# Loading q and k by pairs of tiles, eight tokens of a head to a partition, in a local-attention and maxout-FFN kernel

## The chip, the cores and the metric

The kernel runs on one core of one Trainium2 chip. The metric is the device time of one execution in microseconds. Engine names are those of the profile: PE (TensorE matmul), PEld (its weight loads), DVE (VectorE), ACT (ScalarE), POOL (GpSimd), SP (SyncE, which issues almost all DMA transfers).

## The reference

Inputs are q, k and v with 4 batches, 8 heads, 768 tokens and head size 64, and four FFN weights. Everything is fp32 at the borders.

```python
def _attn_ref(q, k, v, n_global, n_local):          # n_global = 8, n_local = 96
    scores = scale * np.matmul(q, k.transpose(0, 1, 3, 2))
    rel = pos[:, None] - pos[None, :]
    is_global = pos[None, :] < n_global
    is_local = (rel >= 0) & (rel < n_local)
    keep = is_global | is_local
    dist = np.where(is_global & ~is_local, n_local, np.abs(rel))
    slopes = 2.0 ** (-8.0 * (np.arange(H) + 1) / H)
    scores = scores - slopes[:, None, None] * dist
    scores = np.where(keep, scores, -1e9)
    a = softmax(scores)                             # written out in the original
    return np.matmul(a, v)

x = attn_out.transpose(0, 2, 1, 3).reshape(B * S, H * D)       # 3072 x 512
h = np.maximum(np.maximum(x @ w1, x @ w2), x @ w3)             # 3072 x 768
out = h @ w_out                                                # 3072 x 512
```

## The kernel before

**Tiles.** The 4 x 768 tokens are 24 tiles of 128 tokens, numbered 0 to 23, six to a batch. Because a query looks at its own and the 95 tokens before it, and at 8 global tokens, a tile's attention needs k and v of its own tile, of the tile before, and the batch's first 8 tokens. The FFN works on chunks of 4, 2, 2, 4, 4, 4, 4 tiles.

**Units and their order.** The program is a list of units, written out by hand in the string `SCHEDULE`. Each unit issues the instructions of one small step. Every engine, and the DMA queue of SP, executes its own instructions strictly in the order of this list, so a unit that waits holds back all that comes after it on the same engine. The letters that matter here (n is a number of a load group, s a part of it, T a tile, g a half of the heads, c a chunk, f a block of 128 FFN columns; the last number mostly chooses the engine for a copy: 0 ACT, 1 DVE, 2 POOL):

- `l n.s` (`load_part`): loads one part of q or k of a group of tiles in the first half of the kernel; the first two parts are loaded ahead of the list. `c n.s.how` (`cast_part`): casts it to bf16. `x n.s.how` (`u_x`): eight 128x128 PE transposes into PSUM and the copy to `qkT`, which holds q and k with the head dimension on partitions. On copies, 0 is ACT and 1 DVE with PSUM pool psT, 2 and 3 the same engines with pool psH, and 4 splits between both.
- `L T`, `C T.0.how`, `X T.how`: the same for one tile in the second half, with 256-byte rows; X with 4 is a DMA transpose. For C, 3 splits the cast between DVE and POOL.
- `v T` and `C T.1.how`: load and cast v. `G` and `V` put the 8 global tokens in place.
- `S T.g.how` (`u_S`): scores of four heads into PSUM and the exponential on ACT into `P`; with how = 1 the bias is added by PE matmuls, otherwise `M T.g` multiplies `P` by a mask on DVE. `B` and `K` make the bias and mask tables at the start.
- `A T.how` (`u_A`): probabilities times v on PE, then reciprocal and product on DVE into `xb`. `T T.how` (`u_XT`): transpose to `xT`, by PE or (4) by DMA.
- `w`, `W`, `o`, `Q`: load and cast the FFN weights. `F c.f.j` (`u_F1`): one FFN product of a chunk (four matmuls), read by ACT for j = 0 and by a maximum on DVE for j = 1 and 2. `O c.tt.how` (`u_F2`): output of one tile, six matmuls, copy and store. `E`: the last chunk's outputs. `D`: matmuls on zeros.

**Load groups.** Tiles 0 to 11 come in groups given by `GROUPS = [[0, 2], [2, 2], [4, 2], [6, 4], [10, 2]]` (first tile, number of tiles). Each part is 512 KB in one transfer; a partition takes 2 (or 4) neighbouring tokens of each of 8 (or 4) heads, so that a row in memory is 512 bytes (or 1 KB). The pool `raw` that receives q and k has 5 buffers.

**Heads.** Neighbouring heads 2j and 2j+1 share one 128-partition column block j of `qkT`, one in each half of the partitions.

**PSUM.** Pools are psS (score and output tiles, tags sp0 and sp1), psH (3 buffers for FFN products) and psT (1 buffer).

Of the kernel before, what the change touches and what calls it, by code (L numbers as in the profile page):

```python
# [25 lines left out]
    K6 K5 D1.2 D4.8 B2.1 B4.1 B7.1 B5.1 l1.0 l1.1 K4 B6.1 v0 B1.0 B3.1 c0.0.1 K1 K3 x0.0.2 K7 B0.1  # L26
    c0.1.1 x0.1.4 G0.2 c1.0.1 c1.1.1 K0 S0.0.1 S1.1.1 M1.1 S1.0.0 G1.2 x1.0.3 S0.1.1 x1.1.0 K2 M0.0
    C0.1.1 M0.1 A0.1 v1 C1.1.2 S2.0.0 M1.0 S2.1.0 G2.1 T0.1 M2.0 S3.0.0 S3.1.1 M3.1 v2 l2.0 c2.0.1
    M2.1 M3.0 C2.1.2 v3 A1.0 x2.0.2 V1.2 G3.2 A2.1 C3.1.2 T1.0 V2.2 l2.1 c2.1.1 A3.0 V3.0 w0.0 T2.0
    w0.1 x2.1.4 T3.1 W0.0.0 S4.0.0 W0.1.1 S4.1.0 w0.2 D3.1 F0.0.0 G4.1 M4.1 M4.0 F0.1.0 F0.1.1  # L30
    W0.2.0 F0.0.1 S5.1.0 w1.0 W1.0.0 W2.0.1 S5.0.0 F0.1.2 v4 C4.1.1 F0.0.2 M5.1 F0.4.0 w1.1 A4.1
    V4.1 W1.1.1 W2.1.1 w1.2 v5 F0.3.0 M5.0 F0.5.0 F0.2.0 F0.2.1 T4.1 F0.3.1 F0.4.1 W1.2.0 F0.2.2
    C5.1.2 A5.1 W2.2.0 F0.3.2 l3.0 F0.5.1 c3.0.0 T5.1 l3.2 c3.2.0 F0.5.2 x3.2.2 l3.1 c3.1.1 x3.0.1
    F1.4.0 F1.1.0 F1.0.0 l3.3 c3.3.0 o0 Q0.0 x3.1.3 F0.4.2 F1.0.1 x3.3.0 F1.2.0 G6.0 F1.2.1 F1.1.1
    l4.1 o1 S6.0.0 S6.1.0 v6 C6.1.2 Q1.1 F1.0.2 F1.5.0 F1.5.1 S7.0.0 S7.1.0 G7.1 F1.4.1 F1.5.2
    c4.1.1 F1.3.0 o2 Q2.0 F1.4.2 M7.1 v7 S8.0.0 M6.1 l4.0 c4.0.0 L12 L14 C7.1.2 v9 v8 L13 M7.0
    S8.1.0 F1.1.2 v11 O0.3.1 v13 v10 M6.0 A7.0 G8.2 F1.3.1 C12.0.0 O0.0.0 v12 x4.1.2 T7.1 A6.0
    O0.1.1 S9.1.0 S9.0.0 V7.1 M8.0 T6.0 x4.0.3 F1.2.2 M8.1 O0.2.1 M9.0 M9.1 C8.1.0 F2.5.0 F2.0.0
    G9.2 S10.0.0 S10.1.0 G10.2 F1.3.2 C9.1.2 F2.0.1 F2.0.2 A8.0 X12.0 F2.2.0 C13.0.3 V8.2 A9.1 X13.4
    T8.4 T9.4 F2.4.0 F2.5.1 C14.0.1 X14.4 v15 F2.4.1 S11.0.0 S11.1.0 O1.1.0 M11.0 M10.1 M10.0 F2.2.1  # L40
    S12.0.0 S12.1.0 F2.2.2 M11.1 F2.5.2 V9.2 C10.1.2 A10.0 V10.1 C11.1.2 L15 O1.0.0 F2.1.0 F2.4.2
    C13.1.2 A11.0 T10.0 F2.1.1 F2.3.0 S13.1.0 G12.0 S13.0.0 L18 T11.1 M12.1 F2.3.1 F2.3.2 M12.0
    G13.2 C15.1.2 L16 v14 C14.1.2 F3.5.0 F3.4.0 F3.4.1 F2.1.2 C12.1.0 M13.1 S14.0.0 M14.0 C15.0.0
    X15.4 S14.1.0 F3.5.1 M13.0 F3.1.0 A12.0 M14.1 F3.4.2 F3.2.0 F3.0.0 A13.0 V13.0 F3.1.1 C16.0.0
    G14.0 F3.2.1 F3.2.2 L19 F3.3.0 C18.0.0 X16.0 L17 F3.1.2 S15.1.0 S15.0.0 C19.0.1 T12.4 G15.0
    F3.3.1 F3.0.1 F3.0.2 X18.4 T13.4 C17.0.0 A14.1 F3.3.2 V14.1 F3.5.2 M15.0 X19.4 S16.0.0 L20 T14.4
    S16.1.0 M16.1 v18 C18.1.2 v17 v16 O2.0.0 X17.4 O3.2.0 S18.0.0 v19 S18.1.0 G16.0 O3.3.0 M15.1
    A15.0 V15.0 O3.1.0 C20.0.1 M18.1 X20.4 T15.0 M18.0 O3.0.0 F4.3.0 A18.0 M16.0 F4.2.0 F4.0.0
# [14 lines left out]
def kernel(  # L63
# [29 lines left out]
    GROUPS = [[0, 2], [2, 2], [4, 2], [6, 4], [10, 2]]  # L93
# [52 lines left out]
    def part(n, s):  # L146

        T0, sz = GROUPS[n]
        jn = {2: 4, 4: 2, 6: 1}[sz]
        a, x = divmod(s, 4 // jn)  # L150
        return divmod(T0, NT) + (sz, a, x * jn, jn)

    def load_part(n, s):

        bb, t0, sz, a, j0, jn = part(n, s)
        r = raw_pool.tile([128, 2 * DM], FP32, name="rawp", tag="raw")
        r = r[:, 0:sz * jn * 128].rearrange("i (h x) -> i h x", h=2 * jn)
        raw["p", n, s] = r
        src = (q, k)[a][bb, 2 * j0:2 * (j0 + jn), t0 * 128:(t0 + sz) * 128, :]
        nc.sync.dma_start(out=r, in_=src.rearrange("h (i e) d -> i h (e d)", e=sz))  # L160
# [19 lines left out]
    def cast_part(n, s, how):  # L180
        bb, t0, sz, a, j0, jn = part(n, s)
        qk = cast_pool.tile([128, 2 * DM], BF16, name="qkp", tag="qkb")
        qk = qk[:, 0:sz * jn * 128].rearrange("i (e h d) -> i e h d", e=sz, d=D)
        qb["p", n, s] = qk
        copies[how](qk, raw["p", n, s].rearrange("i h (e d) -> i e h d", e=sz))  # L185

    def cast(T, what, how):
        b, t = divmod(T, NT)
        if what == 1:
            va[T] = va_first[b % 2] if t == 0 else va_ring[T % NVA]  # L190
            copies[how](heads(va[T])[:, :, 0:D], rawv[T])  # L191
            return
        qk = cast_pool.tile([128, 2 * DM], BF16, name="qkb", tag="qkb").rearrange("p (a c) -> p a c", a=2)
        qb[T] = qk
        flat = raw[T].rearrange("p a h d -> p a (h d)")
        if how == 3:
            nc.vector.tensor_copy(qk[:, 0], flat[:, 0])
            nc.gpsimd.tensor_copy(qk[:, 1], flat[:, 1])
        else:
            copies[how](qk, flat)  # L200
# [27 lines left out]
    def u_x(n, s, how):  # L228
        bb, t0, sz, a, j0, jn = part(n, s)
        dst = batch_T(bb)[:, a, j0:j0 + jn, t0 * 128:(t0 + sz) * 128].rearrange("c j (i e) -> c j i e", e=sz)  # L230
        if how >= 4 and jn > 1:
            m = jn // 2
            halves = [(0, m, psT, "tp", nc.scalar.copy), (m, jn, psH, "h", nc.vector.tensor_copy)]
        else:
            pool, tag = (psH, "h") if how in (2, 3) else (psT, "tp")
            halves = [(0, jn, pool, tag, copies[how % 2])]
        tps = [pool.tile([128, sz, hi - lo, 128], BF16, name="tpp", tag=tag) for lo, hi, pool, tag, copy in halves]
        for (lo, hi, pool, tag, copy), tp in zip(halves, tps):
            for e in range(sz):
                for j in range(lo, hi):  # L240
                    nc.tensor.transpose(tp[:, e, j - lo],  # L241
                                        qb["p", n, s][:, e, 2 * j:2 * j + 2].rearrange("i h d -> i (h d)"), identb)
        for (lo, hi, pool, tag, copy), tp in zip(halves, tps):

            copy(dst[:, lo:hi], tp.rearrange("c e j i -> c j i e"))  # L245
# [24 lines left out]
    def u_S(T, g, how):  # L270
# [9 lines left out]
        for ds in range(2 if t else 1):  # L280
            for j2 in range(2):
                jp = 2 * g + j2
                for hh in range(2):
                    hsl = slice(64 * hh, 64 * hh + 64)
                    nc.tensor.matmul(sp[:, hh, j2, ds], qT(T - ds, 1)[hsl, jp], qT(T, 0)[hsl, jp],  # L285
                                     start=not how, stop=True, skip_group_check=True)
# [26 lines left out]
    def u_A(T, how):  # L313
# [3 lines left out]
        for g in range(2):  # L317
            P = Pt[T, g]
            for j2 in range(2):
                for hh in range(2):  # L320
                    h = 4 * g + 2 * j2 + hh
                    i = 2 * hh + j2
                    o = op[:, g, (2 * j2 + hh) * 65:(2 * j2 + hh) * 65 + 65]
                    nc.tensor.matmul(o, P[:, i, 0], heads(va[T])[:, h], start=True, stop=(t == 0),  # L324
                                     skip_group_check=True)
                    if t:
                        nc.tensor.matmul(o, P[:, i, 1], heads(va[T - 1])[:, h], start=False, stop=True,  # L327
                                         skip_group_check=True)
# [185 lines left out]
```

## Time and profile before

| quantity | value |
|---|---|
| median of 3 runs | 179.47 us (179.23 to 179.76) |
| the profiled execution's own time | 179.17 us |
| its span, first to last instruction | 177.4 us |
| mean granted TensorE clock | 0.990 of full speed |
| instructions | 3967 |
| HBM read, written | 25.17 MB, 6.29 MB |

A page of the profile gives the busy time of every engine and its share of the span, a strip of 40 equal slices (4.4 us each) with busy tenths, the DMA queues, the chain of work that ended last, and groups of like instructions. In tables by window, each engine has a column with busy microseconds and, in brackets, its number of instructions, in the order PE, PEld, DVE, ACT, POOL; then come the granted PE clock, the DMA share and GB/s. In lists by time, the columns are start, duration, engine and line. The trace also has a record of every DMA packet with its size and duration, and of every landing.

### The profile page before, as it was taken

The page shows a single profiled execution, that of the slowest core. Times are in us where ns is not written, and L with a number is a line of the kernel's source. Part 1 is how long each engine was busy: PE and PEld are TensorE (multiplying, and loading weights), DVE is VectorE, ACT ScalarE, POOL GpSimd, SP SyncE. Part 2 cuts the span into 40 slices and gives each one's busy share as a digit, 9 for nine tenths or more (in the row PEclk, how much of TensorE's full clock was granted, in tenths as well). Part 3 has the DMA queues.
Part 4 walks back from the last instruction along what each step waited for, and adds up shares of the span by engine and source line. Part 5 has one row for each costly group of instructions (what it writes and reads, how often), then busy time and mean ns, then how long its engine had stood idle before and what let it go on. Part 6 is the DMA issues. An engine that isn't in the chain of part 4 may idle for free.

```text
span 177.4 us, 3967 instructions
## 1 busy us (share of the span) xinstructions
PE 170.6 (96%) x1550; PEld 95.7 (54%) x1550; DVE 126.5 (71%) x248; ACT 109.7 (62%) x166; POOL 19.9 (11%) x46
## 2 busy tenths in 40 slices
PE   7586899999999999999999999999999999999997
PEld 2344645458766786855554555455454555444444
DVE  4678969889697999769677557597667597435710
ACT  4979998758797967677595667615456630132022
POOL 4022300100130171010100011101000020000000
PEclk9879999999999999999999999999999999999999
DMA  5999999999999999899999999997796015600006
GB/s 146 291 234 271 344 343 381 321 356 325 289 211 221 241 301 147 214 242 204 213 175 186 208 245 248 231 164 148 176 300 91 0 33 134 218 32 0 4 21 215
DMA packets 85730, 36.04 MB, mean 203 GB/s; under 512 B 68304, under 2 KB 80464, under 8 KB 85712
## 3 DMA queue, kind: packets, MB, share of 16 engines
q1 hardware_dynamic: 85568, 35.73, 86.4%
q8 instruction: 12, 0.20, 0.5%
q10 hardware_dynamic: 144, 0.07, 0.1%
q14 instruction: 6, 0.05, 0.1%
HBM read 25.17 MB, written 6.29 MB: 177 GB/s over the span
## 4 chain that ended last, share of the span: by engine, by line
PE 90%; DMA 3%; issue 2%; ACT 2%; DVE 2%; SPq 0%; POOL 0%
PE h L363 54%; PE po L378 18%; PE sp L285 7%; DMA rawp<-in_k_dram 3%; PE op L324 3%; PE op L327 2%; PE tpp L241 2%; PE wp L440 2%; ACT P L290 1%; PE xtp L351 1%; PE sp L277 1%; DVE xb L334 1%; DVE qkp L185 1%; ACT qkT L245 1%; PE tp L263 1%
## 5 line engine op out<-in xcount | busy, mean ns | idle before, releaser
L363 PE MATMUL h<-xT,w 128*128 128x512 bf16 (+1 forms) x504 | 100.6, 349 | 0.0
L363 PEld LDWEIGHTS <-w 128*128 128x128 bf16 x504 | 46.9, 98 | 40.6 <-ACT w L429 0.2
L290 ACT ACTIVATE P<-sp 128x1024 bf16<-128x1024 f32 (+1 forms) x48 | 43.9, 956 | 12.3 <-PE sp L285 12.1
L368 ACT CAST h<-h 128x512 bf16<-128x512 f32 (+1 forms) x42 | 21.8, 529 | 30.8 <-PE h L363 29.0
L370 DVE TENSOR_TENSOR h<-h,h 128x512 bf16<-128x512 bf16 (+1 forms) x42 | 25.3, 608 | 14.9 <-PE h L363 10.4
L378 PE MATMUL po<-wo,ht 128*128 128x512 bf16 (+2 forms) x156 | 33.4, 363 | 0.0
L309 DVE TENSOR_TENSOR P<-P,wmask 128x1024 bf16<-128x1024 bf16 x38 | 25.4, 686 | 6.1 <-ACT P L290 5.8
L372 DVE TENSOR_TENSOR ht<-h,h 128x512 bf16<-128x512 bf16 (+1 forms) x42 | 25.5, 606 | 5.2 <-PE h L363 4.0
L378 PEld LDWEIGHTS <-ht 128*128 128x128 bf16 x156 | 14.2, 98 | 13.9
L334 DVE TENSOR_TENSOR xb<-op,rz 128x512 bf16<-128x512 f32 x24 | 16.6, 691 | 0.8
L384 ACT COPY ost<-po 128x512 f32<-128x512 f32 (+2 forms) x15 | 8.2, 555 | 14.5 <-PE po L378 14.4
L285 PE MATMUL sp<-qkT 64*128 64x128 bf16 x352 | 15.1, 221 | 0.9 <-ACT qkT L245 0.5
L285 PEld LDWEIGHTS <-qkT 64*128 64x128 bf16 x352 | 10.3, 96 | 9.8 <-issue 6.6
L324 PEld LDWEIGHTS <-P 128*128 128x128 bf16 x192 | 12.5, 97 | 3.6 <-DVE ht L372 0.5
L191 POOL CAST va<-rawv 128x512 bf16<-128x512 f32 x14 | 9.6, 692 | 41.0 <-DMA rawv<-in_v_dram 16.5
L384 DVE COPY ost<-po 128x512 f32<-128x512 f32 (+1 forms) x11 | 7.2, 653 | 9.2 <-PE po L378 9.1
L324 PE MATMUL op<-va,P 128*128 128x65 bf16 x160 | 12.5, 193 | 0.1
L327 PEld LDWEIGHTS <-P 128*128 128x128 bf16 x160 | 10.4, 97 | 1.5
L327 PE MATMUL op<-va,P 128*128 128x65 bf16 x128 | 9.9, 193 | 0.3 <-POOL va L223 0.3
L241 PE MATMUL tpp<-identb,qkp 128*128 128x128 bf16 x96 | 7.6, 227 | 2.2 <-DVE qkp L185 2.2
L245 ACT COPY qkT<-tpp 128x1024 bf16<-128x1024 bf16 (+1 forms) x8 | 7.3, 916 | 2.0 <-PE tpp L241 2.0
L241 PEld LDWEIGHTS <-qkp 128*128 128x128 bf16 x96 | 6.1, 101 | 3.8 <-DVE qkp L185 3.0
(65 smaller groups left out, 108.8 us busy)
## 6 DMA issues: line engine op xcount, KB each, us to landing
rawv<-in_v_dram SPq DMA_DIRECT2D x24, 256.0 KB, 5.3
out_dram<-ost SPq DMA_DIRECT2D x23, 256.0 KB, 3.7
rawp<-in_q_dram SPq DMA_DIRECT2D x6, 512.0 KB, 7.2
rawp<-in_k_dram SPq DMA_DIRECT2D x6, 512.0 KB, 7.2
wst<-in_moe_w_dram SPq DMA_DIRECT2D x3, 1024.0 KB, 10.8
raw<-in_q_dram SPq DMA_DIRECT2D x12, 256.0 KB, 5.3
raw<-in_k_dram SPq DMA_DIRECT2D x12, 256.0 KB, 5.1
wst<-in_moe_w_dram SPq DMA_DIRECT2D x3, 512.0 KB, 7.4
```

The lines of the kernel that those rows point to most:

```text
L241: nc.tensor.transpose(tp[:, e, j - lo], qb["p", n, s][:, e, 2 * j:2 * j + 2].rearrange("i h d -> i (h d)"), identb)
L285: nc.tensor.matmul(sp[:, hh, j2, ds], qT(T - ds, 1)[hsl, jp], qT(T, 0)[hsl, jp], start=not how, stop=True, skip_group_check=True)
L290: nc.scalar.activation(P[:, :, 0:n], sp.rearrange("p a b d n -> p (a b) d n")[:, :, 0:n], AF.Exp, bias=0.0, scale=scale)
L309: nc.vector.tensor_mul(P, P, wmask[:, g, :, 0:2])
L324: nc.tensor.matmul(o, P[:, i, 0], heads(va[T])[:, h], start=True, stop=(t == 0), skip_group_check=True)
L327: nc.tensor.matmul(o, P[:, i, 1], heads(va[T - 1])[:, h], start=False, stop=True, skip_group_check=True)
L334: nc.vector.tensor_tensor(out=x.rearrange("p (g h) d -> p g h d", g=2), in0=o4[:, :, :, 0:64], in1=rz[:, :, :, None].to_broadcast([128, 2, ...
L363: nc.tensor.matmul(ps, w123[f // 2][:, dm, j, (f % 2) * 128:(f % 2) * 128 + 128], xT[c][:, dm], start=(dm == 0), stop=(dm == 3))
L368: nc.scalar.copy(h01, ps)
L370: nc.vector.tensor_max(h01s[c, f], h01s[c, f], ps)
L372: nc.vector.tensor_max(ht[c][:, f], h01s[c, f], ps)
L378: nc.tensor.matmul(po, ht[c][:, f, tt * 128:(tt + 1) * 128], wo[:, f, cols], start=(f == 0), stop=(f == NF - 1))
```

## The change

Tiles 0 to 11 are now six groups of two tiles (n = 0 to 5), each with two parts: s = 0 is q, s = 1 is k. A part is loaded by two transfers of 256 KB. Each takes four heads (z = 0: heads 0 to 3, z = 1: heads 4 to 7); in it a partition holds eight neighbouring tokens of one head, 2 KB in one row, and 32 partitions hold the 256 tokens of a head. After the PE transposes, head h and head h + 4 share a column block, so the pairing of heads changes everywhere: in the bias and mask tables, in scores and outputs, and in the casts of tiles 12 to 23, which now permute heads. `SCHEDULE` is a new list with the same numbers of units of each letter; in it 14 instead of 13 T units and 11 instead of 10 X units are DMA transposes, and 3 instead of 4 S units add the bias on PE.

```diff
-    GROUPS = [[0, 2], [2, 2], [4, 2], [6, 4], [10, 2]]
+    ET = 8
...
     def load_part(n, s):
-        bb, t0, sz, a, j0, jn = part(n, s)
-        r = raw_pool.tile([128, 2 * DM], FP32, name="rawp", tag="raw")
-        r = r[:, 0:sz * jn * 128].rearrange("i (h x) -> i h x", h=2 * jn)
+        b, t0 = divmod(2 * n, NT)
+        r = raw_pool.tile([128, 2 * DM], FP32, name="rawp", tag="raw").rearrange("p (z x) -> p z x", z=2)
         raw["p", n, s] = r
-        src = (q, k)[a][bb, 2 * j0:2 * (j0 + jn), t0 * 128:(t0 + sz) * 128, :]
-        nc.sync.dma_start(out=r, in_=src.rearrange("h (i e) d -> i h (e d)", e=sz))
+        src = (q, k)[s][b, :, t0 * 128:(t0 + 2) * 128, :]
+        for z in range(2):
+            nc.sync.dma_start(out=r[:, z], in_=src[4 * z:4 * z + 4].rearrange("h (i e) d -> h i (e d)", e=ET))
...
     def cast_part(n, s, how):
-        copies[how](qk, raw["p", n, s].rearrange("i h (e d) -> i e h d", e=sz))
+        copies[how](qk, raw["p", n, s].rearrange("p z (e d) -> p e z d", e=ET))
...
     def cast(T, what, how):
-        flat = raw[T].rearrange("p a h d -> p a (h d)")
+        dst = qk.rearrange("p a (j z d) -> p a j z d", z=2, d=D)
+        src = raw[T].rearrange("p a (z j) d -> p a j z d", z=2)
...
     def u_x(n, s, how):
+        tp = pool.tile([128, ET, NP, 128 // NP], BF16, name="tpp", tag=tag)
+        for e in range(ET):
+            nc.tensor.transpose(tp[:, e].rearrange("c j i -> c (j i)"),
+                                qb["p", n, s][:, e].rearrange("p z d -> p (z d)"), identb)
+        copies[how % 2](dst, tp.rearrange("c e j i -> c j i e"))
...
     def u_A(T, how):
-                    h = 4 * g + 2 * j2 + hh
+                h = 4 * (i // 2) + 2 * g + i % 2
```

The new list up to the first FFN unit, the transfers l0.0 and l0.1 having been issued ahead of it:

```
B3.1 B0.1 K7 K0 D0.0 B6.1 B2.1 D2.2 B7.1 l1.1 c0.0.1 B4.1 K4 c0.1.1 l1.0 B1.1 K2 K6 K5 K3 D3.8
B5.1 D4.1 x0.0.1 c1.1.2 x0.1.2 G0.1 K1 S0.1.1 M0.1 S0.0.0 x1.1.3 S1.1.0 c1.0.2 S1.0.0 G1.0 v0
C0.1.2 M0.0 x1.0.1 A0.1 l2.0 c2.0.0 S2.0.1 M1.0 S2.1.0 G2.1 M1.1 x2.0.1 v2 S3.0.0 S3.1.1 G3.0 v1
l2.1 M2.1 c2.1.1 C1.1.2 v3 C2.1.2 A1.0 V1.2 T0.0 M3.0 M2.0 A2.1 V2.0 x2.1.0 M3.1 C3.1.2 w0.0
W0.0.0 A3.0 T1.1 T2.0 T3.1 S4.0.0 w0.1 W0.1.1 w0.2 W0.2.1 S4.1.0 F0.0.0
```

And on to the last load part of tiles 0 to 11 (shortened):

```
F0.0.1 ... w1.0 ... v4 ... w1.1 ... w1.2 ... v5 l3.1 ... l4.0 ... c3.1.0 x3.1.2 l3.0 c3.0.1 F0.2.2
o1 T5.0 Q1.0 F0.5.2 v6 ... o0 l4.1 c4.0.1 ... l5.0 o2 v7 ... v8 l5.1 F1.0.0 L13 F1.2.0 x3.0.0 v10 L12
F1.0.1 F1.3.0 F1.0.2 S6.0.0 S6.1.0 F1.3.1 c4.1.1 F1.1.0 ... F1.2.1 v14 Q2.1 v9 F1.4.0 x4.1.0 x4.0.2
A6.1 C8.1.2 c5.0.1 O0.0.1 M7.0 M7.1 F1.4.1 c5.1.1 F1.2.2 L14 ...
```

More of the change, by code (lines that the diff above doesn't have):

```diff
@@ L31 @@
[L31 to L36, printed above, removed]
@@ new lines @@
+    F0.5.2 v6 o0 l4.1 c4.0.1 G6.2 C6.1.2 l5.0 o2 v7 C7.1.2 v8 l5.1 F1.0.0 L13 F1.2.0 x3.0.0 v10 L12
+    F1.0.1 F1.3.0 F1.0.2 S6.0.0 S6.1.0 F1.3.1 c4.1.1 F1.1.0 M6.0 M6.1 S7.0.0 S7.1.0 G7.0 F1.3.2 Q0.1
+    F1.2.1 v14 Q2.1 v9 F1.4.0 x4.1.0 x4.0.2 A6.1 C8.1.2 c5.0.1 O0.0.1 M7.0 M7.1 F1.4.1 c5.1.1 F1.2.2
+    L14 S8.0.0 S8.1.0 G8.2 C10.1.2 L15 O0.1.0 v13 A7.0 F1.5.0 M8.1 x5.1.2 F1.1.1 S9.1.0 S9.0.0
+    F1.4.2 T7.1 F1.5.1 M9.1 v11 F1.5.2 T6.0 x5.0.3 v12 O0.2.0 F2.1.0 C12.0.3 F2.1.1 M8.0 V7.2 G9.2
@@ new lines @@
+    F3.4.0 O2.0.0 S15.1.0 S15.0.0 F3.3.0 M15.0 O2.1.1 A14.1 V14.0 C19.0.3 F3.1.2 F3.0.0 C15.1.0
+    M15.1 A12.1 T12.4 F3.3.1 F3.4.1 F3.5.0 A15.1 F3.5.1 G15.0 F3.4.2 C16.1.1 S16.0.0 V15.0 S16.1.0
+    T14.4 T15.4 v17 F3.0.1 F3.5.2 F3.0.2 F3.3.2 L18 X19.4 v19 G16.0 S17.0.0 S17.1.0 M16.1 M16.0
+    C17.1.1 F4.3.0 F4.4.0 C18.0.3 C18.1.2 M17.1 M17.0 F4.0.0 F4.0.1 A16.1 F4.1.0 F4.3.1 F4.1.1 V16.2
+    L20 C20.0.3 A17.0 X18.4 L21 T17.4 O3.0.1 L22 v21 X20.4 C19.1.1 F4.4.1 F4.1.2 F4.5.0 S19.1.0
+    S19.0.0 F4.5.1 F4.3.2 C21.0.1 F4.4.2 M19.0 S18.0.0 M18.0 M19.1 S18.1.0 M18.1 F4.2.0 O3.2.1
@@ L59 @@
+    F5.1.2 F5.5.2 V22.2 A23.0 T23.4 O5.0.0 O5.1.0 O5.2.0 O4.2.0 F6.2.0 F6.4.0 F6.2.1 O4.3.1 F6.2.2
+    F6.3.0 F6.1.0 O5.3.0 F6.5.0 F6.5.1 F6.4.1 F6.1.1 F6.1.2 F6.3.1 F6.0.0 F6.3.2 F6.0.1 F6.0.2
+    F6.4.2 F6.5.2 E D1.2
 """
@@ L194, in cast @@
         qb[T] = qk
-        flat = raw[T].rearrange("p a h d -> p a (h d)")
+        dst = qk.rearrange("p a (j z d) -> p a j z d", z=2, d=D)
+        src = raw[T].rearrange("p a (z j) d -> p a j z d", z=2)
         if how == 3:
-            nc.vector.tensor_copy(qk[:, 0], flat[:, 0])
-            nc.gpsimd.tensor_copy(qk[:, 1], flat[:, 1])
+            nc.vector.tensor_copy(dst[:, 0], src[:, 0])
+            nc.gpsimd.tensor_copy(dst[:, 1], src[:, 1])
         else:
-            copies[how](qk, flat)
+            copies[how](dst, src)
     def batch_T(b):
@@ L228, in u_x @@
     def u_x(n, s, how):
[L229 to L245, printed above, removed]
+        b, t0 = divmod(2 * n, NT)
+        dst = batch_T(b)[:, s, :, t0 * 128:(t0 + 2) * 128].rearrange("c j (i e) -> c j i e", e=ET)
+        pool, tag = (psH, "h") if how in (2, 3) else (psT, "tp")
+        tp = pool.tile([128, ET, NP, 128 // NP], BF16, name="tpp", tag=tag)
[3 more added lines that the diff above has]
+        copies[how % 2](dst, tp.rearrange("c e j i -> c j i e"))
     def u_X(T, how):
@@ L280, in u_S @@
         for ds in range(2 if t else 1):
[L281 to L285, printed above, removed]
+            for i in range(2):
+                jp = 2 * g + i
+                for z in range(2):
+                    hsl = slice(64 * z, 64 * z + 64)
+                    nc.tensor.matmul(sp[:, z, i, ds], qT(T - ds, 1)[hsl, jp], qT(T, 0)[hsl, jp],
                                      start=not how, stop=True, skip_group_check=True)
@@ L318, in u_A @@
             P = Pt[T, g]
-            for j2 in range(2):
-                for hh in range(2):
-                    h = 4 * g + 2 * j2 + hh
-                    i = 2 * hh + j2
-                    o = op[:, g, (2 * j2 + hh) * 65:(2 * j2 + hh) * 65 + 65]
-                    nc.tensor.matmul(o, P[:, i, 0], heads(va[T])[:, h], start=True, stop=(t == 0),
+            for i in range(4):
+                h = 4 * (i // 2) + 2 * g + i % 2
+                o = op[:, h // 4, (h % 4) * 65:(h % 4) * 65 + 65]
+                nc.tensor.matmul(o, P[:, i, 0], heads(va[T])[:, h], start=True, stop=(t == 0),
+                                 skip_group_check=True)
+                if t:
+                    nc.tensor.matmul(o, P[:, i, 1], heads(va[T - 1])[:, h], start=False, stop=True,
                                      skip_group_check=True)
-                    if t:
-                        nc.tensor.matmul(o, P[:, i, 1], heads(va[T - 1])[:, h], start=False, stop=True,
-                                         skip_group_check=True)
         x = xb_pool.tile([128, H, D], BF16, name="xb", tag="xb")
```

62 lines of the change are left out of this document (21 added, 41 removed).

## The prediction

> **What bounds the kernel now.** I read the page first, then the chain of waits, the windows and SP's timeline.
>
> ```profile
> span 177.4 us, 3967 instructions
> ...
> PE 170.6 (96%) x1550; PEld 95.7 (54%) x1550; DVE 126.5 (71%) x248; ACT 109.7 (62%) x166; POOL 19.9 (11%) x46
> ...
> DMA  5999999999999999899999999997796015600006
> ...
> q1 hardware_dynamic: 85568, 35.73, 86.4%
> ```
>
> TensorE is busy 96%, but the one load queue is nearly as full: the DMA row stands at 9 or 8 until slice 27 (about 120 us). Two resources are close to their limits.
>
> ```profile
> 0.74 0.45 SPq L160
> ...
> 1.25 5.46 DMA rawp<-in_k_dram
> ...
> 6.74 0.70 DVE qkp L185
> ...
> 21.88 0.40 PE xtp L351 x4
> ...
> 23.19 0.90 PE h L363 x4
> ```
>
> The start of the chain: k of tiles 0 and 1 lands at 6.7 us, and until 23.2 us four tiles go through attention, with short PE pieces between ACT and DVE work. Then come the long FFN groups (L363), and the windows show no gap any more:
>
> ```profile
> 23.00:60.00 37.00, 36.99 (x358) 23.03 (x358) 31.43 (x61) 30.57 (x43) 3.13 (x5) 1.00 1.09 299
> 60.00:100.00 40.00, 40.00 (x435) 24.78 (x434) 31.03 (x62) 29.18 (x47) 6.27 (x11) 1.00 1.06 213
> ```
>
> The second column is PE. So: the time is the start (about 23 us), 151 us of dense PE (22.9 to 174.1 in the chain) and 3.3 us to the end of the span. It grows one for one with whatever delays the first FFN group or opens a gap later.
>
> What a load costs, by windows in which one row length prevails (512 B; 1 KB; 2 KB; last column GB/s):
>
> ```profile
> 4.00:8.00 4.00, 2.01 (x17) 1.16 (x16) 2.97 (x9) 3.63 (x8) 0.00 (x0) 0.92 1.21 296
> ...
> 18.50:22.00 3.50, 2.72 (x54) 2.12 (x51) 3.17 (x7) 3.14 (x7) 1.32 (x4) 1.00 1.09 351
> 28.00:30.00 2.00, 2.00 (x17) 1.00 (x16) 1.77 (x5) 1.97 (x4) 0.00 (x0) 1.00 1.05 387
> ```
>
> 2-KB rows run at 387 GB/s, 24.2 GB/s for each of 16 engines. Rows of 256 B (v) run at 218 in the window 11 to 12.5 us. The packet records agree: a 2-KB packet lasts 92 ns on average, 81 at least.
>
> **The step that decides: how many engines carry a new load.** All 118 transfers of the trace end in 16 landing records each (1888 in all), one per engine. Every load and store among them has 128 partitions as the outermost dimension on both sides. The new source is `h (i e) d -> h i (e d)`: outermost are 4 heads, 49,152 elements apart, which do not merge with the 32 rows inside. No row of the trace shows such a pattern, so the cost has two ends: 16 engines, 256 KB / 387 GB/s = 0.68 us; or 4 engines, 64 KB each at 24.2 GB/s = 2.71 us. What tells between them is how the issuer deals out a transfer:
>
> ```profile
> 0.74 0.45 SPq L160 DMA_DIRECT2D rawp<-in_q_dram  x1
> ...
> 174.42 0.37 ACTq L385 DMA_DIRECT2D out_dram<-ost  x1
> ```
>
> The first issue hands out 1024 rows, the last store 128, and 0.45 against 0.37 us says that rows are not dealt one by one. The issuer cuts the pattern into a few equal shares, and the simplest cut is along the outermost dimension: 128 gives 16 shares, 4 heads give 4. I take 4 engines, and as all 24 new transfers have the same shape, the same four each time (nothing in the instruction would choose others).
>
> The Trainium skill ("DMA: Bandwidth & Descriptors", "Why a DMA increments its semaphore by 16 and not by 1") says it outright: the engine count is the largest number up to 16 that divides the outermost counts of both patterns, and this queue takes the lowest-numbered ones. By it this load costs 2.71 us, by the 16 landing records of every load so far 0.68; no run here shows it yet.
>
> **The sum with four engines.** All loads share one queue in order, so a transfer has landed when these four are through with everything ahead. Work of one of them: a new load part (two transfers) 128 KB / 24.2 = 5.42 us; a v load 16 KB at 13.6 GB/s = 1.20; w of the first kind 32 KB at 21.9 = 1.49; of the second 2.71; wo 1.35. The first bytes move at 1.95 us (packet records); landing is told 0.85 us after the last packet (k of tiles 0 and 1: 5.85 against 6.7). In the new order l0.0 is through at 7.4, l0.1 12.8, l1.1 18.2, l1.0 23.6, v0 24.8, l2.0 30.3, v2 and v1 32.7, l2.1 (k of tiles 4 and 5) 38.1, landed 39.0.
>
> The cast c2.1 waits for l2.1 on DVE. Behind it on DVE stand A1's reciprocal and product, M3.0, those of A2 and A3, T1, T3: by rows 0.61 (cast) + 3 x 0.9 + 0.61 + 2 x 0.4 = 4.7 us, and PE's first FFN group waits for T3. First FFN group: 43.7 us against 23.2. The weights are no later (w0.0 lands at 41.7).
>
> Then v3, w, v4, v5 to 54.3, and the next parts: l3.1 59.7, l4.0 65.1, l3.0 70.6, wo and v6 74.5, l4.1 79.9, l5.0 85.3, wo, v7, v8 89.1, l5.1 94.5. PE would reach x3.0 at about 64, yet c3.0 stands on DVE ahead of F0.2.2's maximum, so the three psH buffers fill and PE stops until 72. The same at c4.1 (81), Q2.1 (88) and c5.1 (96.1 with landing and cast): the loads pace everything until then.
>
> After c5.1 the PE queue still holds 72 wide groups x 0.863 + 25 narrow x 0.433 + 23 output tiles x 1.29 + 16 score tiles x 0.55 (two of them half) + 17 A x 0.49 + 2.25 of transposes = 121.5 us; the same sum over all dense work of before gives 149.6 against 151.2 measured, so 122.7. That has one X and one T transpose less on PE (0.67 us). After the stalls the clock can fall as it did between 5 and 11 us (mean 0.72): 3.4 us at half, 1.7 lost. The 256-B loads that follow start right at 95, with some 8 us less lead over PE than before (L12 landed about 10 us before its use); of 0 to 8 I take 2, since L12 still comes in time by the order. Sum: 96.1 + 122.7 + 1.7 + 2 + 3.3 = 225.8 of span; 179.17 - 177.4 = 1.8 outside it: 227.6; the median before lies 0.3 above its profiled run: **227.9**.
>
> **The other edits, which this hides.** The casts of tiles 12 to 23 now permute heads in 64-element runs: the row with such runs (L185 on DVE, 686 ns) is no dearer than the flat one (L200, 745). Copies L245 gather eight tokens instead of two or four: 1.03 us on ACT, 1.22 on DVE for both old forms, so 0 +- 0.1 each. c1.0 and c1.1 go to POOL, two halves of 0.69 each: 1.4 us apiece, before tiles 2 and 3. Before the first FFN group ACT loses 1.2 us of work, DVE gains 0.9. Twelve more issues on SP, 0.45 us each, fit in a queue that waits for the engines. The head pairing leaves every S and A matmul its size.
>
> **Rivals.** *A, all 16 engines carry the loads (faster).* Then k of tiles 0 and 1 lands 1 MB x (1/296 - 1/387) = 0.8 us sooner, tiles 2 and 3 1.7. Following the queues with the rows: l1.1 lands at 7, POOL's cast to 8.5, x1.1 on DVE to 10.7, x1.0 to 12.2, the last of eight exponentials ends at 16.6 (18.7 before), A3 at 20, first FFN group at 20.9: 2.2 saved, 0.7 less on PE: 179.5 - 2.9 = 176.6 (175.5 to 178.5). For it: the landing records. It decides if rows are dealt flat. The skill's same page (Specifications) puts line rate at 512 B and more; by that the longer rows would save nothing and A would give 177.4 or more, but 296 against 387 GB/s here speaks against it.
> *B, four engines, but others for each transfer.* Four transfers then run side by side: full rate later, while the first q and k take up to 2 us more. This eats A's gain: 178 to 180.
>
> **Chances and range.** Four fixed engines 0.85: one cut along the outermost dimension is what the issue times point to, against landing records that fit both. A 0.11, B 0.04 (half of it no change). The forecast's own range: 2-KB packets at 92 ns +5.7, more lag +6, clock again +1.7: 242. Downward: all packets at the shortest of their kind (81, 44, 15 ns) -5.7, no lag, no clock loss -3.7; packets overlapping as in the window 4 to 8 us (share 1.21) some -6 more: 212. That holds 0.95 of 0.85. About 0.3% is what a measurement of this kernel can tell from no change; so slower 0.86, faster 0.12, same 0.02.
>
> **What would show it.** Right: the new loads land some 5 us apart per part; DVE's c lines wait for DMA rawp; GB/s falls to near 100 in the first 20 us; first L363 at about 44 us; PE gaps at 63 to 96, dense after. Wrong: rawp landings of 4 us or less, early GB/s near 380, and L363 near 21 us (A). If the loads are slow but the end lies far off 228, the error is in the rate of one engine or in the lag after 95 us.

## The result and the profile after

| | before | after |
|---|---|---|
| median (lowest to highest) of 4 runs each, same chip | 179.53 us (179.23 to 179.76) | 229.38 us (228.81 to 229.53) |
| profiled execution, its span | 179.17, 177.4 us | 228.81, 227.0 us |
| mean granted TensorE clock | 0.990 | 0.879 |

The ratio is 1.277 (1.274 to 1.280): slower by 28%. Forecast were 227.9 us, in a range of 212 to 242. Ratios leave out executions that took over 1.5% more than the fastest of the same kernel; where that drops many, the median of all of them is given beside it.

The page of after, in the order in which the page of before was read (busy times; the strip of the DMA engines, with GB/s below it; the load queue; the chain that ended last, by engine):

```profile
span 227.0 us, 3940 instructions
...
PE 180.0 (79%) x1527; PEld 101.1 (45%) x1527; DVE 127.3 (56%) x251; ACT 101.6 (45%) x158; POOL 26.1 (12%) x54
...
DMA  1242447898266274459999999799948951342005
GB/s 49 99 123 97 120 118 179 274 329 289 96 179 166 91 179 123 115 138 231 249 257 134 238 238 196 192 218 213 232 116 173 264 121 60 77 166 90 3 4 185
...
q1 hardware_dynamic: 79904, 36.12, 67.4%
...
PE 53%; DMA 23%; SPq 18%; DVE 2%; issue 1%; ACT 1%; POOL 0%; DVEq 0%; ACTq 0%; POOLq 0%
```

No engine gained work worth the 50 us: PE is 9 us busier, POOL 6, DVE and ACT hardly change or fall. Nearly the same bytes went through the same queue (35.73 MB before, 36.12 MB now), but where the DMA strip of before began with 5 and then nines, this one begins with 1242447, and in the second to sixth slices (5.7 to 34 us) it moves 97 to 123 GB/s. The chain that sets the end is now 41% DMA and SP's queue.

Windows of after (length, then PE, PEld, DVE, ACT, POOL, granted clock, DMA share, GB/s):

```profile
4.00:14.00 10.00, 2.66 (x13) 1.20 (x11) 2.08 (x7) 2.75 (x7) 0.00 (x0) 0.72 0.26 99
60.00:97.00 37.00, 21.72 (x181) 13.83 (x180) 15.53 (x31) 12.47 (x19) 2.21 (x5) 0.77 0.51 138
97.00:140.00 43.00, 40.24 (x449) 26.23 (x448) 32.49 (x70) 28.18 (x45) 8.36 (x15) 1.00 1.09 210
140.00:180.00 40.00, 38.85 (x326) 19.13 (x325) 29.63 (x55) 18.01 (x28) 5.13 (x10) 1.00 1.05 200
```

Between 4 and 14 us only the new loads are on their way. A DMA share of 0.26 of 16 engines is 4.2 engines, and 99 GB/s is four times 24.7. In 60 to 97 us PE works 21.7 of 37 us; after 97 us it is dense again.

Some of the casts of the new loads on DVE, and one cast of an FFN weight (L412) among the later ones, by time (start, duration, and in brackets how long the engine had stood idle and for what):

```profile
9.03 0.69 DVE L177 CAST qkp<-rawp 128x1024 bf16<-128x1024 f32 x1 [3.91 <-DMA rawp<-in_q_dram]
14.37 0.69 DVE L177 CAST qkp<-rawp 128x1024 bf16<-128x1024 f32 x1 [4.38 <-DMA rawp<-in_k_dram]
...
41.70 0.69 DVE L177 CAST qkp<-rawp 128x1024 bf16<-128x1024 f32 x1 [4.97 <-DMA rawp<-in_k_dram]
...
75.21 0.69 DVE L177 CAST qkp<-rawp 128x1024 bf16<-128x1024 f32 x1 [10.06 <-DMA rawp<-in_q_dram]
...
92.75 0.69 DVE L412 CAST wo<-wost 128x1024 bf16<-128x1024 f32 x1 [4.46 <-DMA wost<-in_moe_w_out_dram]
100.98 0.69 DVE L177 CAST qkp<-rawp 128x1024 bf16<-128x1024 f32 x1 [3.78 <-DMA rawp<-in_k_dram]
```

The first two are 5.3 us apart: the time of one part on four engines. The last cast, c5.1, starts at 100.98 us. And PE, at its first FFN group and at two of its gaps:

```profile
47.49 3.70 PE L343 MATMUL h<-xT,w 128*128 128x512 bf16 x12
...
76.55 1.01 PE L343 MATMUL h<-xT,w 128*128 128x256 bf16 x4 [9.45 <-DVE ht L352]
...
102.06 0.61 PE L227 MATMUL tpp<-identb,qkp 128*128 128x128 bf16 x8 [2.66 <-DVE ht L352]
```

The gap of 9.45 us at 76.55 is named after `ht` (L352), a maximum on DVE that reads an FFN product. But DVE was not busy: it stood for 10.06 us at c3.0, ahead of that maximum in its queue, waiting for q of tiles 6 and 7. The load is the cause, and PE's row shows only its last link.

### The profile page after: what moved, and what is told of

Same layout as the page of the kernel before. It is cut to its first block, busy times and chain, and to the rows that moved or that the text cites. A ratio compares the mean times of both kernels' runs of the same rounds, so it can differ in the third digit from the quotient of the medians.

```text
span 227.0 us, 3940 instructions
## 1 busy us (share of the span) xinstructions
PE 180.0 (79%) x1527; PEld 101.1 (45%) x1527; DVE 127.3 (56%) x251; ACT 101.6 (45%) x158; POOL 26.1 (12%) x54
## 3 DMA queue, kind: packets, MB, share of 16 engines
q1 hardware_dynamic: 79904, 36.12, 67.4%
## 4 chain that ended last, share of the span: by engine, by line
PE 53%; DMA 23%; SPq 18%; DVE 2%; issue 1%; ACT 1%; POOL 0%; DVEq 0%; ACTq 0%; POOLq 0%
PE h L343 31%; DMA rawp<-in_k_dram 15%; PE po L358 13%; SPq L153 8%; DMA rawp<-in_q_dram 7%; SPq L399 5%; PE sp L269 3%; SPq L404 2%; SPq L169 2%; DMA xT<-xb 2%; PE op L304 2%; PE op L307 1%; PE tpp L227 1%; DVE qkT L229 1%; DVE P L291 1%
## 5 line engine op out<-in xcount | busy, mean ns | idle before, releaser
L343 PE MATMUL h<-xT,w 128*128 128x512 bf16 (+1 forms) x504 | 105.1, 357 | 10.6 <-DVE ht L352 9.5
L274 ACT ACTIVATE P<-sp 128x1024 bf16<-128x1024 f32 (+1 forms) x48 | 43.3, 954 | 24.6 <-PE sp L269 24.5
L358 PE MATMUL po<-wo,ht 128*128 128x512 bf16 (+2 forms) x156 | 35.1, 371 | 3.0 <-DVE wo L412 3.0
L348 ACT CAST h<-h 128x512 bf16<-128x512 f32 (+1 forms) x42 | 21.7, 529 | 27.8 <-PE h L343 27.8
L227 PE MATMUL tpp<-identb,qkp 128*128 128x128 bf16 x96 | 10.6, 278 | 27.1 <-DVE qkp L177 13.9
L352 DVE TENSOR_TENSOR ht<-h,h 128x512 bf16<-128x512 bf16 (+1 forms) x42 | 25.0, 606 | 5.0 <-PE h L343 4.3
L177 DVE CAST qkp<-rawp 128x1024 bf16<-128x1024 f32 x8 | 5.7, 715 | 30.7 <-DMA rawp<-in_k_dram 16.8
L227 PEld LDWEIGHTS <-qkp 128*128 128x128 bf16 x96 | 8.2, 125 | 29.7 <-DVE qkp L177 17.6
L364 ACT COPY ost<-po 128x512 f32<-128x512 f32 (+2 forms) x18 | 10.0, 560 | 19.3 <-PE po L358 18.7
L229 ACT COPY qkT<-tpp 128x1024 bf16<-128x1024 bf16 x7 | 7.1, 1012 | 19.7 <-PE tpp L227 19.7
L304 PEld LDWEIGHTS <-P 128*128 128x128 bf16 x192 | 13.8, 104 | 3.0 <-DVE P L291 0.8
L304 PE MATMUL op<-va,P 128*128 128x65 bf16 x160 | 13.5, 199 | 0.5 <-DVE P L291 0.5
L229 DVE COPY qkT<-tpp 128x1024 bf16<-128x1024 bf16 x5 | 6.1, 1221 | 12.6 <-PE tpp L227 12.6
L307 PEld LDWEIGHTS <-P 128*128 128x128 bf16 x160 | 11.4, 102 | 1.7
```

The costliest lines, as they stand in the source:

```text
L227: nc.tensor.transpose(tp[:, e].rearrange("c j i -> c (j i)"), qb["p", n, s][:, e].rearrange("p z d -> p (z d)"), identb)
L274: nc.scalar.activation(P[:, :, 0:n], sp.rearrange("p a b d n -> p (a b) d n")[:, :, 0:n], AF.Exp, bias=0.0, scale=scale)
L343: nc.tensor.matmul(ps, w123[f // 2][:, dm, j, (f % 2) * 128:(f % 2) * 128 + 128], xT[c][:, dm], start=(dm == 0), stop=(dm == 3))
L348: nc.scalar.copy(h01, ps)
L352: nc.vector.tensor_max(ht[c][:, f], h01s[c, f], ps)
L358: nc.tensor.matmul(po, ht[c][:, f, tt * 128:(tt + 1) * 128], wo[:, f, cols], start=(f == 0), stop=(f == NF - 1))
```

## The experiments

Theory 1 is the prediction's: the outermost dimension of four heads deals each load to four fixed engines. Theory 2 puts the loss elsewhere: in the new queue order, the doubled number of transfers, or the rows themselves.

### Is it the pattern, and how does the time depend on it?

**rows_outermost.** The same rows of 2 KB, the same queue order, the same number of transfers; only which partition takes which row is turned round, so that 32 rows are outermost in the pattern and the heads inside:

```diff
-            nc.sync.dma_start(out=r[:, z], in_=src[4 * z:4 * z + 4].rearrange("h (i e) d -> h i (e d)", e=ET))
+            nc.sync.dma_start(out=r[:, z], in_=src[4 * z:4 * z + 4].rearrange("h (i e) d -> i h (e d)", e=ET))
...
-        tp = pool.tile([128, ET, NP, 128 // NP], BF16, name="tpp", tag=tag)
+        tp = pool.tile([128, ET, 128 // NP, NP], BF16, name="tpp", tag=tag)
...
-            nc.tensor.transpose(tp[:, e].rearrange("c j i -> c (j i)"),
+            nc.tensor.transpose(tp[:, e].rearrange("c i j -> c (i j)"),
...
-        copies[how % 2](dst, tp.rearrange("c e j i -> c j i e"))
+        copies[how % 2](dst, tp.rearrange("c e i j -> c j i e"))
```

**two_heads.** Each transfer of the change is cut in two, of two heads each, into 64 partitions. By theory 1 the divisor is now 2:

```diff
+            for y in range(2):
-                nc.sync.dma_start(out=r[:, z], in_=src[4 * z:4 * z + 4].rearrange(...))
+                nc.sync.dma_start(out=r[64 * y:64 * y + 64, z], in_=src[4 * z + 2 * y:4 * z + 2 * y + 2].rearrange("h (i e) d -> h i (e d)", e=ET))
```

**one_head.** Eight transfers to a part, one head each; the pattern is then 32 rows of one head:

```diff
-        for z in range(2):
-            nc.sync.dma_start(out=r[:, z], in_=src[4 * z:4 * z + 4].rearrange("h (i e) d -> h i (e d)", e=ET))
+        for h in range(H):
+            nc.sync.dma_start(out=r[32 * (h % 4):32 * (h % 4) + 32, h // 4], in_=src[h].rearrange("(i e) d -> i (e d)", e=ET))
```

Expected of rows_outermost:

> The changed kernel with one thing turned round: a load's partitions are ordered by row, then head, so that the outermost dimension of the source counts 32 instead of 4; the copy out of PSUM puts the columns back. Bytes, row length (2 KB), number of transfers, queue order, head pairing and casts stay. Theory (a transfer is dealt along its outermost dimension, 4 heads = 4 engines): all 16 engines carry the loads, early rate some 380 instead of 98 GB/s, first FFN group near 21 us, 176.6 us (175.5 to 178.5). Rival (2-KB rows by head, the new queue order, the casts on POOL or the head pairing are slow in themselves): within 5 us of 229. Rival B (four engines, others for each transfer) is already against the trace after, where several transfers in a row together run at 98 GB/s.

Expected of two_heads:

> The changed kernel with each 256-KB load cut into two of two heads (64 partitions each): the outermost dimension counts 2. Theory: two engines, 49 GB/s in the first 20 us, a part takes 10.84 us instead of 5.42; l2.1 through at 70.6 us, first FFN group near 76, l5.1 through near 160, time about 292 us (280 to 300). Rival (the cost hangs on the rows moved, not on how many engines share them): a part still takes 5.4 us and the time stays near 229.

Expected of one_head:

> The changed kernel with one transfer of 64 KB per head: the outermost dimension is now the 32 rows of the head, and there are 96 load transfers instead of 24. Theory: all 16 engines carry each, so the data take 1.35 us a part, but eight issues at some 0.5 us on SP make 4 us a part: l2.1 lands near 28 us, first FFN group near 33, the last part near 61, time about 193 us (186 to 205). Rival (loads by head with 2-KB rows are slow in themselves, or more and smaller transfers cost more): 229 us or more.

Measured: rows_outermost 179.84 us (178.52 to 181.6, 12 runs), against before 1.000 (0.997 to 1.004); two_heads 290.52 us and one_head 205.22 us (one run each). The stretch that showed four engines in after, in rows_outermost (first) and in two_heads:

```profile
4.00:14.00 10.00, 7.56 (x71) 4.97 (x70) 6.94 (x15) 7.09 (x14) 2.64 (x3) 0.83 1.04 288
```

```profile
4.00:14.00 10.00, 2.06 (x5) 0.45 (x3) 1.12 (x5) 2.75 (x7) 0.00 (x0) 0.79 0.12 47
```

Outermost 2, 4 and 32 give DMA shares of 0.12, 0.26 and 1.04 and 47, 99 and 288 GB/s: about two engines, four, and all. The landing records count them: each new transfer leaves 5 in after, one soon after its issue and four as its data land; it leaves 3 in two_heads, and 16 in rows_outermost and in one_head. The bytes, their rows and the queue order are the same in all three, and rows_outermost issues as many transfers as after. So the 49.5 us between 229.38 and 179.84 come from the outermost count alone. The order of rows on the partitions had no price in return: the eight transposes write the other order and the copies read it, and the copies (L229) take 1.01 us on ACT and 1.22 on DVE in both kernels.

one_head came out just above the range expected of it. Its first FFN group came at 33.6 us as thought, so the early loads went as theory 1 has it. But SP now had 96 issues in place of 24, of 0.42 us each by their median, and where they stood behind the FFN weights they did not get ahead: l5.1 was issued only at 68.9 to 74 us and its cast started at 75.69, where I had 62. The loads were then late because SP issued them late, and not for want of engines: between 50 and 70 us the DMA share is 0.60 to 0.62.

### Early loads or late ones?

**rows_outermost_first_half.** Groups 0 to 2 with rows outermost, groups 3 to 5 as changed (shortened; the copy out of PSUM follows in groups 0 to 2):

```diff
...
+                "h (i e) d -> i h (e d)" if n < 3 else "h (i e) d -> h i (e d)", e=ET))
...
```

> The load groups 0 to 2 (tiles 0 to 5, all before the first FFN group) with rows outermost, groups 3 to 5 (tiles 6 to 11) with the 4 heads outermost as in the changed kernel. Theory with the prediction's sum (loads set the pace until the last of them is cast): six parts save 5.42 - 1.35 = 4.07 us each, 24.4 us in all; the last part is through near 70 us and the time is about 205 us (200 to 209), with PE gaps before c3.0, c4.1, c5.1. Rival (the later loads lie beside FFN work and only the start costs): 177 to 181 us.

Measured 205.26 us (205.18 to 206.22), 1.143 (1.136 to 1.150) against before, as the theory had it. Its first FFN group stands at 24.1 us, as in rows_outermost, and yet half of the loss is there. Its last load cast:

```profile
76.45 0.69 DVE L178 CAST qkp<-rawp 128x1024 bf16<-128x1024 f32 x1 [3.75 <-DMA rawp<-in_k_dram]
```

From the start of the last load cast to the end of the execution, this kernel took 128.8 us (205.21 - 76.45), after 127.8, two_heads 127.8 (290.52 - 162.69), one_head 129.5. Over 85 us of difference in time, what follows c5.1 stays within 1.7 us. The end is set by when the last slow load lands.

### Where did the gain of longer rows go?

With all engines at work, rival A forecast 176.6 us; rows_outermost gives before's time. Its row for k of tiles 0 and 1, its first FFN group, and the start of its loads (window):

```profile
7.48 0.70 DVE L177 CAST qkp<-rawp 128x1024 bf16<-128x1024 f32 x1 [1.49 <-DMA rawp<-in_k_dram]
...
24.23 1.02 PE L343 MATMUL h<-xT,w 128*128 128x512 bf16 x4
...
4.00:6.00 2.00, 2.00 (x7) 0.67 (x6) 1.99 (x7) 2.00 (x6) 0.00 (x0) 1.00 0.90 250
```

k comes 0.7 us later than before (6.74), not 0.8 sooner, and the 2-KB rows run at 250 GB/s here, although later, at 28 to 30 us, the same kernel reaches 386. (This profiled execution took 181.07 us, longer than the kernel's median of 179.84.) Three suspects: the queue order, the load on DVE up to the first FFN group, and the issues on SP, of which the first parts now need two each (at least 0.595 us apiece, where before issued 512 KB in 0.45 and 0.56). Three kernels follow, all on rows_outermost:

**rows_outermost_old_queue**: before's `SCHEDULE`, with its load units renamed (l3.0 stays, l3.1 to l4.0, l3.2 to l3.1, l3.3 to l4.1, l4 to l5, and their c and x; a copy split in two goes to ACT). **less_on_dve**: x1.0.1 to x1.0.0, c2.1.1 to c2.1.2, G2.1 to G2.0, T1.1 to T1.0, that is from DVE to ACT or POOL. **k_from_act_queue** issues k of tiles 0 and 1 from ACT's queue instead of SP's:

```diff
-            nc.sync.dma_start(out=r[:, z], in_=src[4 * z:4 * z + 4].rearrange("h (i e) d -> i h (e d)", e=ET))
+            (nc.scalar if (n, s) == (0, 1) else nc.sync).dma_start(out=r[:, z], in_=src[4 * z:4 * z + 4].rearrange("h (i e) d -> i h (e d)", e=ET))
```

> The kernel rows_outermost (2-KB rows, 16 engines, heads paired h and h+4) with the queue order of the kernel before, its units of tiles 6 to 11 renamed to the new groups (and copies that were split between ACT and DVE given to ACT). rows_outermost came out level with before (179.8 against 179.5), while rival A of the prediction had it at 176.6. Theory 1: the new queue order is what eats the gain of the longer rows (DVE is full from 11 to 23 us in it); then the old order gives 177 to 178.5. Theory 2: the longer rows gain nothing at the start (k of tiles 0 and 1 is cast at 7.5 us instead of 6.7); then the old order gives 179 to 180.5.

> rows_outermost with four units of the start taken from DVE: the copies of x1.0 and T1 to ACT, the cast c2.1 and the copy of G2 to POOL and ACT: 2.3 us off DVE, 1.6 on ACT. Theory: DVE's queue between 11 and 23.5 us sets the first FFN group (24.2 us); it comes 1 to 1.5 us sooner, 178.3 to 179 us. Rival: ACT (9.9 of 12 us busy there) becomes the bound: no change or slower, 179.5 to 181.

> rows_outermost with the two transfers of l0.1 (k of tiles 0 and 1) issued by ACT instead of SP, so that they don't stand behind two others on SP at 0.6 us each. Theory: the four issues of the first tiles at 0.6 us on one engine are what makes k late; k is cast at some 6.5 instead of 7.5 us and the first FFN group comes 0.5 to 1 us sooner, 179 us. Rival: the transfers share the same engines, and DVE's work from 11 us on sets the start: no change (179.8 +- 0.4), or later, since ACT's first work waits for the issues.

The old queue order: 181.48 us (180.75 to 183.66), ratio 1.012 (1.009 to 1.016). It is a little worse with these loads than the new order, so the new order did not eat the gain; the time fits neither theory. Less on DVE: 180.7 us, 1.009 (1.006 to 1.012). DVE's busy time between 11 and 23 us fell from 10.88 to 8.64 us as meant, and no time was gained. The first FFN group came at 25.4 us, but the granted clock between 11 and 23 us was 0.72 in this execution and 0.88 in that of rows_outermost, so the row by itself does not clear DVE. k from ACT's queue: 179.63 us, but in its profiled execution (177.83 us) q was cast at 6.0, k at 6.9, and the first FFN group came at 22.1. That seemed to point to the issues, so it was run again, with two neighbours: both edits together, and the ACT issue in before's own kernel (l0.1, 512 KB, one transfer).

> Both of the last two edits together. If both theories hold: first FFN group near 22.5 us, 177.5 to 178.5 us, below both kernels of the case. If neither: 180.

> The kernel k_from_act_queue once more: its six executions went from 176.9 to 180.4 us, too wide to call. Theory: with the issue of k on a second engine the first loads run at 396 instead of 250 GB/s (4 to 6 us) and the first FFN group starts near 22.1 us, so the median lies 1 to 2 us below the kernel before, with the spread of the early clock on top. Rival: the low two were chance; median 179.5 to 180.

> The kernel before, with the one transfer of its second load part (k of tiles 0 and 1) issued by ACT. There the issues (0.45 and 0.56 us for 512 KB each) were ahead of the data. Theory: no change, within 0.3% of 179.3, which makes the issue time a cost of the change's doubled transfers. Rival: any earlier issue of k helps, 178.5 or less.

Together: 179.68 us, 1.003 (1.000 to 1.007), no gain. k_from_act_again: 179.53 us in the median of twelve, no better than before's 179.19; its ratio, 0.991 (0.988 to 0.995), rests on the six shortest of the twelve. Its trace takes back what the first one seemed to show. The window from 11 to 23 us and the first FFN group of k_from_act_queue, and then of k_from_act_again, which is the same kernel:

```profile
11.00:23.00 12.00, 9.62 (x160) 6.25 (x156) 11.26 (x21) 11.25 (x16) 3.80 (x6) 1.00 1.10 320
...
22.09 2.75 PE L343 MATMUL h<-xT,w 128*128 128x512 bf16 x11
```

```profile
11.00:23.00 12.00, 10.36 (x154) 7.22 (x153) 10.52 (x19) 10.42 (x15) 2.15 (x5) 0.80 1.09 316
...
23.90 2.75 PE L343 MATMUL h<-xT,w 128*128 128x512 bf16 x12
```

The loads are as early in both (q is cast at 6.0 and 6.1 us, k at 6.9 and 7.0), yet the first FFN group of the second comes 1.8 us later. In it the granted clock is 0.80 instead of 1.00, and two bias operations on DVE (L280) take 1.46 us from 7.58 on, where they took 0.62; how the 1.8 us divide was not followed. So one execution's first FFN group does not tell what the issues are worth, and no gain in time is established for this edit. What holds in every trace is the rate of the 2-KB loads between 4 and 6 us: 387 to 409 GB/s in the four with issues on SP and ACT (z1_from_act, below, among them), 248 to 252 in the three with SP alone (rows_outermost, less_on_dve, rows_outermost_old_queue).

before_k_from_act: 180.19 us, 1.007 (1.003 to 1.010), a little more than the 0.3% that was allowed. With one transfer to a part, sharing the issues gained nothing: q was cast at 6.24 us instead of 5.32, k at 7.17 instead of 6.74. That fits the issues being a price of the change's own doubled transfers, and does not prove it.

**z1_from_act** shares them another way: of q and of k of tiles 0 and 1, heads 0 to 3 are issued by SP and heads 4 to 7 by ACT, at the same time.

```diff
-            nc.sync.dma_start(out=r[:, z], in_=src[4 * z:4 * z + 4].rearrange("h (i e) d -> i h (e d)", e=ET))
+            (nc.scalar if n == 0 and z else nc.sync).dma_start(out=r[:, z], in_=src[4 * z:4 * z + 4].rearrange("h (i e) d -> i h (e d)", e=ET))
```

> rows_outermost with the second transfer of each of l0.0 and l0.1 issued by ACT, so that q and k of tiles 0 and 1 each come from both issuers at once. Theory: the first four issues overlap two by two, q and k are both cast by 6.9 us, as in k_from_act_queue: 177.5 to 179. Rival: no gain over rows_outermost, 179.8.

Measured 178.64 us (177.49 to 180.5, 12 runs) beside 179.19 for before (28 runs): 0.996 (0.993 to 0.999). Its rows that answer to those above:

```profile
6.25 0.69 DVE L177 CAST qkp<-rawp 128x1024 bf16<-128x1024 f32 x1 [0.25 <-DMA rawp<-in_k_dram]
...
21.96 2.75 PE L343 MATMUL h<-xT,w 128*128 128x512 bf16 x12 [0.96 <-ACT xT L332]
...
4.00:6.00 2.00, 1.48 (x9) 0.55 (x8) 2.00 (x7) 2.00 (x6) 0.00 (x0) 1.00 1.05 387
```

With two issuing engines the same 2-KB loads run at 387 GB/s in place of 250, and k is cast at 6.25, 0.5 us sooner than before. The cause is shown as far as this: two of the first four issues moved, and the rate rose by half. Why single packets last longer (up to 1.1 us) when SP issues alone stays open: an issue each 0.63 us of 256 KB would still allow some 415 GB/s. The first FFN group comes 1.2 us sooner than before, but the granted clock was 1.00 from 5 to 23 us in this execution and 0.72 between 5 and 11 us in that of before, so the 1.2 us are not the issues' alone. About 0.5 us reach the median.

This kernel has the lowest median of the study: what the change does, with the rows outermost and the first issues shared, is 0.4% ahead of before. That this is a gain is not settled: of the executions with a mean granted clock of 1.00, the eight of this kernel have a median of 178.5 us and the ten of before 178.8.

## Why the prediction was right, and where it was not

**Four fixed engines: right, and shown.** Share 0.26 and 99 GB/s in after, 0.12 and 47 with two heads, 1.04 and 288 with rows outermost. (The issue times that it leaned on were a weak sign: 128 rows take some 0.6 us to issue here, before's 1024 rows took 0.45.) Rival A is out by the first figure. Rival B, four engines that change from transfer to transfer, would have had several transfers side by side and a higher rate over 4 to 14 us, when one load followed the other at a steady 99 GB/s; it is out too. The Trainium skill's rule ("DMA: Bandwidth & Descriptors", "Why a DMA increments its semaphore by 16 and not by 1") agrees with all three: the largest number up to 16 that divides both outermost counts is 2, 4 and 16.

**The size of a part: right.** 5.42 us forecast, 5.34 between the first two casts; one engine moved 24.7 GB/s between 4 and 14 us, where I took 24.2. That is the size with the four engines alone at work.

**The landing times: the term that was mis-sized.** The start of the cast against the forecast landing: 9.0 and 8.2 for l0.0, 14.4 and 13.7 for l0.1, 41.7 and 39.0 for l2.1, 75.2 and 71.5 for l3.0, 101.0 and 95.4 for l5.1. The lag grows from 0.8 to 5.6 us. The first part of it is the beginning: I let the four engines start at 1.95 us, where the first packet of before began, but in after only 54 packets of 2 KB went between 2 and 4 us, as much as four engines do in 1.1 us; so 2.9 would have been the right start.

The rest is the term "64 KB each at 24.2 GB/s = 2.71 us", which the sum takes for every new load alike. By the packet records it holds while the four engines work alone: between 17.5 and 24 us 312 packets of 2 KB move, 24.6 GB/s an engine at 87 ns a packet, and l0.1 takes 5.3 us from its first packet to its last. While the other twelve engines carry v or weights, the four move less: 15.4 GB/s an engine between 15.5 and 17 us (137 ns a packet), 17.9 between 35 and 39 us (122 ns). So l1.1, beside v0, takes 5.9 us, l2.1, beside v3 and the first weights, 7.2, and l5.1, beside the loads behind it, 6.7. Why the engines slow each other stays open. The range had a price for longer packets (92 ns, +5.7), the forecast itself had none.

One might think instead that SP's late issues let the four engines run dry, since the packets of 2 KB all but stop (6 of them between 32 and 34 us):

```profile
32.00:34.00 2.00, 0.17 (x2) 0.17 (x3) 0.00 (x0) 1.27 (x2) 0.00 (x0) 0.50 0.32 66
```

But a share of 0.32 is 5.1 engines at work. Between 31.6 and 34.0 us 512 packets of 256 B move, just the four engines' quarter of v2 and v1 (1024 packets each), and of v1's 16 landings twelve come at 31.1 to 31.7 us and four at 34.2 to 34.9. The four engines were on their shares of v, which the sum has at 1.20 us each. Between 91.5 and 94.1 us they are on v7 and v8 in the same way.

**The first FFN group: 47.5 us, forecast 43.7.** Of the 3.8 us, 2.7 are the late landing of l2.1. The other 1.1 is DVE's chain from c2.1 to T3: 5.8 us, where I added 4.7 from rows.

**After c5.1: too much, and it paid for the landings.** c5.1 was done at 101.7, forecast 96.1 (+5.6). From there to the last output product (218.01 + 5.37 = 223.4) were 121.7 us; I had 122.7 + 1.7 + 2 = 126.4 (-4.7). The 1.7 for the clock was not paid: it is 1.00 in 97 to 140 and in 140 to 180 us. It was lower before, 0.77 in 60 to 97 us, when PE waited for loads in any case. The largest item is work that I counted behind c5.1 and that PE had done while DVE still waited, since PE's queue need not stop where DVE's does: F1.2.2, both halves of S8, O0.1, A7 and F1.5.0 were through by 99.4 us, 3.2 us by the prices of the sum. The 2 us for less lead of the 256-B loads were not paid as such: PE stood idle for 1.6 us in the 121.7, 1.0 of it for a DMA transpose (`xT`, at 148.3 us), and no wait that the profile lists there is for such a load. (The 2.8 us in 97 to 140 are nearly all the wait for c5.1 itself, which ends at 102.06.) The remainder, some 0.6 us the other way, is work that took longer than its price. With 0.3 more at the end, 225.8 became 227.0. So the sum is right to 0.5% by luck, with two errors of some 5 us against each other; a reader should trust the mechanism more than that agreement.

**The gaps: right in place, and two of the four for the reason told.** PE stops at c3.0, c4.1, Q2.1 and c5.1. At c3.0 and c5.1 DVE stands at a cast ahead of a maximum (L352) that PE's buffers need. At c4.1 (2.50 us, ending at 86.42) and Q2.1 (2.95, ending at 93.49) PE waits for what the cast itself writes, `qkp` and `wo`.

**The edits said to be free: right.** The gathers of eight tokens (L229, `qkT` from PSUM) take 1.01 us on ACT and 1.22 on DVE, against 1.03 and 1.22 before. A POOL cast of a whole part (128x1024) takes 1.04 us, not the 1.4 that I added from two halves.

**Rival A's own sum: wrong, and unseen by the outcome.** Its -2.9 us rests on 387 GB/s from the first transfer. With all engines at work it came out as 0. The step that failed is "Twelve more issues on SP, 0.45 us each, fit in a queue that waits for the engines": an issue took 0.6 us, and in the first 6 us, where there is no lead yet, the rate hangs on how many engines issue. That is a part of it only: with two issuing engines and a granted clock of 1.00, z1_from_act still starts its first FFN group at 21.96 us where A had 20.9, and its median is 178.64 where A had 176.6. What else A's sum had wrong stays open. The Trainium skill ("DMA: Bandwidth & Descriptors", "Specifications") puts line rate at 512 B and more, by which the longer rows would have saved nothing: the time came out so, but not for that reason, since where the transfers are fed the rates are 387 and 296 GB/s.

## What to carry to other kernels

Before a load is re-cut for longer rows, look at the outermost count of both its patterns and put a dimension there that keeps all DMA engines at work; here the same bytes to another order of partitions is the difference between 229 and 180 us. When the first loads are several small transfers, issuing them from two engines' queues can be tried: here it raised their rate from 250 to 387 GB/s, but a gain in time was not established, and with one larger transfer to a part there was none. When one queue in order feeds engines that work in order, add up when the last slow load lands and what is left to do after it: that sum held here over 85 us of difference. In such a sum the rate of an engine that works alone (24.6 GB/s) is too high for the stretches in which the others work beside it (15.4 and 17.9 in the two stretches above).

## What the runs showed of the hardware that was not expected

- A load of 256 KB with a pattern of 32 x 4 rows of 2 KB takes about 0.6 us to issue, more than before's 512 KB of 1024 rows of 512 B (0.45 and 0.56). Between 4 and 6 us the 2-KB loads run at 248 to 252 GB/s with one issuing engine and at 387 to 409 with two.
- Nothing rebalances a load of few engines: in 10 us of after, 12 of 16 DMA engines had next to nothing to do, while the same queue held the next transfers. Where the others do work, the few are slower: 15.4 instead of 24.6 GB/s an engine.
- One kernel shows a mean granted clock of 0.998 in one profiled execution (k_from_act_queue, 177.83 us) and 0.981 in another (k_from_act_again, 180.53 us); the twelve runs of the latter, on one chip, go from 176.82 to 180.69 us, and the first FFN group of the two profiled executions starts at 22.1 and 23.9 us. That spread is larger than the 0.4% in question, so a small gain can't be read from one run.
